# Loads cut into four pieces per partition row, and the tenth step's load and the constants issued earlier

## The chip, the core and the metric

The kernel runs on one core of one Trainium2 chip. The metric is the device time of one execution in microseconds (us), less is better. Its engines are named as in the profile: PE is TensorE's matmuls and PEld its weight loads, DVE is VectorE, ACT is ScalarE, POOL is GpSimd, SP is SyncE. Each engine works through its own instructions in order and waits on semaphores for the others. All loads and stores are issued by SP and carried by 16 DMA engines.

## What is computed

A retention layer (attention without softmax, with a decay of its own in each head) is followed by a feed-forward layer with softplus. Everything is float32:

```python
batch, n_heads, seq, head_dim = (8, 8, 576, 64)          # q, k, v
scores = q @ k.transpose(0, 1, 3, 2) / sqrt(64)
gamma = 1.0 - 2.0 ** (-5.0 - arange(8))
ret = scores * where(rel >= 0, gamma[:, None, None] ** rel, 0.0)   # rel = i - j
x = (ret @ v).transpose(0, 2, 1, 3).reshape(4608, 512)
h = x @ w_in                                             # w_in 512 x 2048
g = maximum(h, 0.0) + log1p(exp(-abs(h)))
return g @ w_out                                         # w_out 2048 x 512
```

## The kernel before

The 4608 tokens are cut into 36 chunks of 128. A **step** m is half of a chunk (four of the eight heads), so there are 72 steps, counted from 0. A step needs 576 KB of q, k and v in one tile, `raw0`, `raw1` and so on (`load_step`, line 118; step 0 comes as two `part` tiles together with constants). A step does `scores` and `sums` on PE (lines 156 and 169), the masked copy `a` and the running states on DVE (lines 178 to 210), then `values` on PE (lines 220 and 231), and `values_out`: x on DVE, its high part on ACT (line 246) and the rest on DVE or POOL (line 247). `scale_values` multiplies v by the decay, on ACT in the steps 0 to 8 (line 148) and on POOL from step 9 on (line 145).

The feed-forward layer goes over 9 units of 512 tokens (8 steps each) and in a unit over 16 slots of 128 hidden columns. A slot i is 12 matmuls `h` (`hidden_mm`, line 262), ACT's abs, exp and ln (lines 270 to 272), DVE's softplus (line 276) and the split of g into two parts (ACT line 280, DVE line 284), and 12 matmuls `y` (`output_mm`, line 296), which stand one slot later. Every product is made of three, from the high and the low parts of both sides.

The weights are 32 pieces of 512 KB (two for each p: w_in and w_out), loaded as float64 bits into `wst` (four buffers, `load_weight`) and turned into float32 high and low parts by `weight_p` (ACT, line 329), `weight_t` and `weight_b` (DVE, lines 336 and 342), `weight_c` (ACT, line 350) and `weight_d` (DVE, line 355). The load of piece n + 4 stands behind `weight_d(n)`.

The order is written by hand. **The opening** does the steps 0 to 8 (`AHEAD` is 9). All their loads and the weight pieces 0 to 3 are issued ahead of its loop; pieces 4 and 5, the loads of steps 9 and 10 and the full constants (`consts_sb`) are issued inside it. SP's loads share eight semaphores, `DMAHW0` to `DMAHW7`, so that each load waits until the one eight places ahead of it has landed. Behind the opening stands slot 0, whose `h` needs the x of steps 0 to 7. Slot 1 and every second slot after it begin with one more step on PE (step 9 in slot 1), ahead of the slot's `h`. The `h` of slot 1 needs weight piece 2, whose low part `weight_d(2)` makes on DVE during slot 0. DVE's order there is `weight_t(2)`, `weight_b(2)`, `weight_t(3)`, `weight_b(3)`, `weight_t(4)`, `weight_d(2)`, softplus.

Of the kernel before, what the change touches and what calls it, by code (L numbers as in the profile page):

```python
# [30 lines left out]
AHEAD = CPU * NPAIR // 2 + 1  # L31
# [8 lines left out]
OPENING = 3  # L40
NOPEN = AHEAD + 2
FIRST_HALF = NF // 2
WBUFS = 4
NPIECE = 2 * NF
HI, LO = 0, 1
# [15 lines left out]
def retention_softplus_ffn(ctx: ExitStack, tc, first, others, consts, w, out):  # L61
    nc = tc.nc
# [8 lines left out]
    openp = open_pools.enter_context(tc.tile_pool(name="openp", bufs=1))  # L71
    wst = weight_pools.enter_context(tc.tile_pool(name="wst", bufs=WBUFS, side="right"))
    later = {}
# [10 lines left out]
    consts_sb = const.tile([P, NCONST], F32, name="consts_sb")  # L84
# [11 lines left out]
    def place_weights(pool, upto):  # L96
        while len(ws) < upto:
            ws.append(pool.tile([P, 2, 2 * PIECE], F32R, name=f"w{len(ws)}"))

    place_weights(wpool, FIRST_HALF)  # L100

# [16 lines left out]
    def load_step(m):  # L118

        if m == 0:  # L120
            at = 0
            for x in parts:
                nc.sync.dma_start(x, first[:, at:at + x.shape[1]])
                at += x.shape[1]
            kq, kv = parts[0][:, 0:KQ], parts[1][:, 0:4 * C]
        else:
            if m < NOPEN:
                r = openp.tile([P, RAW], F32, name=f"raw{m}")
            else:
                r = rawp.tile([P, RAW], F32, tag="rawp", name="rawp")  # L130
            nc.sync.dma_start(r, others[m - 1])
            kq, kv = r[:, 0:KQ], r[:, KQ:]
        k = kq[:, 0:2 * C].rearrange("p (s c) -> p s c", s=2)
        q = kq[:, 2 * C:].rearrange("p (s c) -> p s c", s=2)
        kv = kv.rearrange("p (a s c) -> p a s c", a=2, s=2)
        live[m] = dict(k=k, q=q, kp=kv[:, 0], v=kv[:, 1])

    def scale_values(m):

        if m >= NSTEP:  # L140
            return
        v = live[m]["v"].rearrange("p s (h d) -> p (s h) d", h=2)
        f = constant[0][0][:, 4 * (m % 2):4 * (m % 2) + 4]
        if m >= AHEAD:
            nc.gpsimd.tensor_mul(v, v, f.unsqueeze(2).broadcast_to([P, 4, D]))  # L145
            return
        for n in range(4):
            nc.scalar.activation(v[:, n], v[:, n], AF.Copy, scale=f[:, n:n + 1])

    def scores(m, bank):  # L150
        if m >= NSTEP:
            return
        L = live[m]
        for s in range(2):
            for t, h in quads:
                nc.tensor.matmul(bank[rows[t], h, SCOLS][:, part[s]], L["k"][rows[h], s, part[t]],  # L156
                                 L["q"][rows[h], s, part[t]], start=True, stop=True, skip_group_check=True)
        L["bank"] = bank

    def sums(m):  # L160

        if m >= NSTEP:
            return
        L = live[m]
        start, follows = _chunk_kind(m // 2)
        for s in range(2):
            for t, h in quads:
                if follows if t else start != HC:
                    nc.tensor.matmul(L["bank"][rows[h], t, TCOLS][:, part[s]], L["kp"][rows[t], s, rows[h]],  # L169
                                     L["v"][rows[t], s, rows[h]], start=True, stop=True, skip_group_check=True)  # L170

    def scores_out(m):

        if m >= NSTEP:
            return
        L = live[m]
        a = moe.tile([P, 2, 2, HC], F32, tag="a", name="a")
        nc.vector.tensor_mul(a.rearrange("p h s c -> p (h s) c"),  # L178
                             L["bank"][:, :, SCOLS].rearrange("p h (s c) -> p h s c", s=2),
                             mask.unsqueeze(1).broadcast_to([P, 4, HC]))  # L180
        L["a"] = a
# [33 lines left out]
    def values(m, bank):  # L215

        L = live[m]
        for s in range(2):
            for t, h in quads:
                nc.tensor.matmul(bank[rows[h], t, VCOLS][:, part[s]], L["v"][rows[t], s, rows[h]],  # L220
                                 L["a"][rows[t], h, s], start=(s == 0), stop=L["states"][t] is None,
                                 skip_group_check=True)
        for s in range(2):
            for t, h in quads:
                if L["states"][t] is None:
                    continue
                if t == h:
                    lhs, rhs = L["states"][t], L["q"][rows[t], s, part[t]]
                else:
                    lhs, rhs = L["sx"], L["q"][rows[t], s, C:QC]  # L230
                nc.tensor.matmul(bank[rows[h], t, VCOLS][:, part[s]], lhs[rows[t], s], rhs, start=False, stop=True,  # L231
                                 skip_group_check=True)

    def values_out(m, bank, rest):

        live.pop(m)
        ch, pr = m // 2, 2 * (m % 2)
        cols = slice((ch % CPU) * C, (ch % CPU + 1) * C)
        hi, lo = (x_tile(ch // CPU)[:, n, pr:pr + 2, cols] for n in (HI, LO))
        x = att.tile([P, 2, C], F32, tag="x", name="x")  # L240
        nc.vector.tensor_mul(x.rearrange("p s (t c) -> p s t c", t=2),  # L241
                             bank[:, :, VCOLS].rearrange("p t (s c) -> p s t c", s=2),
                             constant[0][2][:, pr:pr + 2].rearrange("p s (t c) -> p s t c", t=2))

        def parts_out():
            nc.scalar.copy(hi, x)  # L246
            rest.tensor_sub(lo, x, hi.bitcast(F32))  # L247
        return parts_out
# [65 lines left out]
    wl = {}  # L314

    def load_weight(n):
        if n < NPIECE:
            wl[n] = wst.tile([P, PIECE, 2], I32, tag="wst", name="wst", bufs=WBUFS)
            nc.sync.dma_start(wl[n].rearrange("p c a -> p (c a)"), w[n // 2, n % 2])

    def weight_a(n):
        weight_p(n)
        weight_t(n)
# [14 lines left out]
    def weight_b(n):  # L338
        if n >= NPIECE:
            return  # L340
        hi, lo = wl[n][:, :, 1], wl[n][:, :, 0]
        nc.vector.scalar_tensor_tensor(hi, hi, 3, lo, op0=ALU.logical_shift_left, op1=ALU.bitwise_or)  # L342
# [5 lines left out]
    def weight_c(n):  # L348
        if n in wl:
            nc.scalar.copy(weight_dst(n)[0], wl[n][:, :, 1].bitcast(F32))  # L350

    def weight_d(n):
        if n in wl:
            head, rest = weight_dst(n)
            nc.vector.tensor_sub(rest, wl.pop(n)[:, :, 1].bitcast(F32), head.bitcast(F32))  # L355

    def weight_dl(n):
        if n in wl:
            weight_d(n)
            load_weight(n + WBUFS)  # L360

# [4 lines left out]
    for m in range(AHEAD):  # L366
        load_step(m)
        for n in first_weights.get(m, ()):
            load_weight(n)
    nc.gpsimd.memset(mask, 1.0)  # L370
    for n in range(2):
        nc.gpsimd.affine_select(out=mask[rows[n]], in_=mask[rows[n]], pattern=[[1, HC]], compare_op=ALU.is_ge,
# [7 lines left out]
    for m in range(AHEAD):  # L380
        pair = ps_open.tile([P, 2, T], F32, tag="pair", name="pair")
        bank = (ps_val if m % 2 else ps_att).tile([P, 2, T], F32, tag="val" if m % 2 else "bank", name="bank")
        if m < AHEAD - 1:
            scores(m, pair)
            sums(m)
        if m > 0:
            values(m - 1, bank)
        if m == AHEAD - 1:
            scores(m, pair)
            sums(m)  # L390
            values_out(m - 1, bank, nc.vector)()
        if m < AHEAD - 1:
            scale_values(m + 1)
        scores_out(m)
        states_out(m)
        if 0 < m < AHEAD - 1:
            values_out(m - 1, bank, nc.gpsimd)()
        if m in (3, 6):
            weight_b((m - 3) // 3)
            weight_c((m - 3) // 3)  # L400
        if m in (4, 7):
            weight_d((m - 4) // 3)
            load_weight((m - 4) // 3 + WBUFS)
        if m in (2, 5, 8):
            weight_a((m - 2) // 3)
        if m == AHEAD - 2:
            load_step(AHEAD)
            nc.sync.dma_start(consts_sb, consts)
            load_step(AHEAD + 1)
    weight_b(2)  # L410
    scale_values(AHEAD)
# [6 lines left out]
    for i in range(NSLOT):  # L418
        n = START_WEIGHTS + 2 * i
        m = AHEAD + (i - 1) // 2  # L420
# [115 lines left out]
```

## Time and profile before

| | us |
|---|---|
| median of three runs | 905.57 (904.87 to 907.06) |
| the profiled execution | 907.14 |
| its span, first to last instruction | 905.4 |
| PE busy in the span | 889.3 (98%) |
| PE idle in the first 40 us | 11.0 |

The profiled execution took 907.14 us, of which the span is 905.4 us. The page lists each engine's busy time, the slices of the span, the DMA queues, and a chain of work that ended last. In the chain PE holds 92%, DVE 4%, DMA 2% and ACT 1%. A table by stretch tells where PE does not work, a timeline of an engine tells what each wait ended with ("<-"), and the DMA view tells what the queues carried in a stretch: queue q1 carries the kernel's loads and stores, q8 and q14 carry instructions. In these profiles a matmul of float32 operands stands as two rows of work, and "issue" is time in which the engine waited for nothing that the profile shows.

### The profile page before, as it was taken

The page shows a single profiled execution, that of the slowest core. Times are in us where ns is not written, and L with a number is a line of the kernel's source. Part 1 is how long each engine was busy: PE and PEld are TensorE (multiplying, and loading weights), DVE is VectorE, ACT ScalarE, POOL GpSimd, SP SyncE. Part 2 cuts the span into 40 slices and gives each one's busy share as a digit, 9 for nine tenths or more (in the row PEclk, how much of TensorE's full clock was granted, in tenths as well). Part 3 has the DMA queues.
Part 4 walks back from the last instruction along what each step waited for, and adds up shares of the span by engine and source line. Part 5 has one row for each costly group of instructions (what it writes and reads, how often), then busy time and mean ns, then how long its engine had stood idle before and what let it go on. Part 6 is the DMA issues. An engine that isn't in the chain of part 4 may idle for free.

```text
span 905.4 us, 18152 instructions
## 1 busy us (share of the span) xinstructions
PE 889.3 (98%) x7826; PEld 724.9 (80%) x7826; DVE 366.4 (40%) x742; ACT 443.3 (49%) x771; POOL 144.9 (16%) x269
## 2 busy tenths in 40 slices
PE   6899999999999999999999999999999999999998
PEld 5677778888888888888888888888888888888886
DVE  5788963333332343333333333323332432332222
ACT  5687764344444444444444444444444444445444
POOL 3312211111111111111111111111111111100000
PEclk9899999999999999999999999999999999999999
DMA  9565623111211131111211131113111121101001
GB/s 362 185 206 199 211 81 100 53 54 54 98 33 49 54 100 54 54 52 38 90 54 53 54 100 53 30 51 101 53 54 54 64 67 50 54 1 47 1 1 46
DMA packets 20527, 70.37 MB, mean 78 GB/s; under 512 B 2272, under 2 KB 2272, under 8 KB 20448
## 3 DMA queue, kind: packets, MB, share of 16 engines
q1 hardware_dynamic: 20448, 69.23, 22.9%
q8 instruction: 61, 1.00, 0.5%
q14 instruction: 18, 0.15, 0.0%
HBM read 59.78 MB, written 9.44 MB: 76 GB/s over the span
## 4 chain that ended last, share of the span: by engine, by line
PE 92%; DVE 4%; DMA 2%; ACT 1%; issue 1%; SPq 0%; DVEq 0%
PE h L262 43%; PE y L296 41%; PE bank L156 3%; PE bank L220 2%; PE bank L231 2%; PE bank L169 2%; DMA raw<-others 1%; DVE w L355 1%; DVE g L284 1%; DMA wst<-w 0%; DVE x L241 0%; DVE a L178 0%; ACT ab L272 0%; ACT ab L271 0%; ACT ab L270 0%
## 5 line engine op out<-in xcount | busy, mean ns | idle before, releaser
L262 PE MATMUL h<-xt,w 128*128 128x512 f32 (+1 forms) x1740 | 426.7, 395 | 0.0
L296 PE MATMUL y<-w,g 128*128 128x512 f32 x1728 | 415.8, 390 | 1.3 <-DVE g L284 1.3
L296 PEld LDWEIGHTS y<-w,g 128*128 128x128 f32 x1728 | 324.0, 188 | 70.7 <-DVE g L284 3.8
L262 PEld LDWEIGHTS h<-xt,w 128*128 128x128 f32 x1740 | 321.8, 189 | 69.1 <-ACT xt L246 0.6
L276 DVE SCALAR_TENSOR_TENSOR ab<-h,ab 128x512 f32<-128x512 f32 (+1 forms) x145 | 99.8, 688 | 427.2 <-ACT ab L272 427.2
L270 ACT ACTIVATE ab<-h 128x512 f32<-128x512 f32 (+1 forms) x145 | 86.3, 595 | 257.6 <-PE h L262 257.6
L280 ACT CAST g<-ab 128x512 fp32r<-128x512 f32 (+1 forms) x145 | 89.5, 617 | 102.5 <-DVE ab L276 101.3
L284 DVE TENSOR_TENSOR g<-ab,g 128x512 fp32r<-128x512 f32 (+1 forms) x145 | 101.3, 699 | 90.6 <-ACT g L280 89.2
L247 POOL TENSOR_TENSOR xt<-x,xt 128x256 fp32r<-128x256 f32 x71 | 54.6, 769 | 470.8 <-ACT xt L246 470.5
L271 ACT ACTIVATE ab<-ab 128x512 f32<-128x512 f32 (+1 forms) x145 | 91.2, 629 | 4.6
L272 ACT ACTIVATE ab<-ab 128x512 f32<-128x512 f32 (+1 forms) x145 | 91.2, 629 | 4.6
L246 ACT CAST xt<-x 128x256 fp32r<-128x256 f32 x72 | 29.2, 406 | 68.3 <-DVE x L241 68.3
L145 POOL TENSOR_TENSOR rawp<-rawp,consts_sb 128x256 f32<-128x256 f32 x61 | 39.9, 655 | 110.2 <-DMA rawp<-others 110.2
L156 PEld LDWEIGHTS bank<-rawp 64*64 64x64 f32 x976 | 19.8, 133 | 21.5 <-issue 21.5
L212 POOL TENSOR_TENSOR s<-s,consts_sb 128x128 f32<-128x128 f32 x55 | 23.9, 435 | 60.5 <-DVE s L210 49.3
L156 PE MATMUL bank<-rawp 64*64 64x64 f32 x976 | 28.2, 231 | 0.0
L350 ACT CAST w<-wst 128x512 fp32r<-128x512 f32 x32 | 21.2, 663 | 13.5 <-DVE wst L342 13.3
L220 PE MATMUL bank<-a,rawp 64*64 64x64 f32 x976 | 27.3, 220 | 0.0
L241 DVE TENSOR_TENSOR x<-bank,consts_sb 128x256 f32<-128x256 f32 x64 | 26.7, 418 | 0.0
L178 DVE TENSOR_TENSOR a<-bank,mask 128x256 f32<-128x256 f32 x63 | 26.2, 416 | 0.0
L231 PE MATMUL bank<-rawp,sx 64*64 64x64 f32 x440 | 25.2, 218 | 0.0
L169 PE MATMUL bank<-rawp 64*64 64x64 f32 x864 | 25.2, 218 | 0.0
(70 smaller groups left out, 411.2 us busy)
## 6 DMA issues: line engine op xcount, KB each, us to landing
rawp<-others SPq DMA_DIRECT2D x61, 576.0 KB, 4.0
wst<-w SPq DMA_DIRECT2D x32, 512.0 KB, 4.1
out<-osb SPq DMA_DIRECT2D x36, 256.0 KB, 2.4
raw<-others SPq DMA_DIRECT2D x10, 576.0 KB, 8.8
part<-first SPq DMA_DIRECT2D x1, 512.0 KB, 3.7
part<-first SPq DMA_DIRECT2D x1, 326.0 KB, 2.9
consts_sb<-consts SPq DMA_DIRECT2D x1, 262.0 KB, 5.8
```

The lines of the kernel that those rows point to most:

```text
L156: nc.tensor.matmul(bank[rows[t], h, SCOLS][:, part[s]], L["k"][rows[h], s, part[t]], L["q"][rows[h], s, part[t]], start=True, stop=True, s ...
L169: nc.tensor.matmul(L["bank"][rows[h], t, TCOLS][:, part[s]], L["kp"][rows[t], s, rows[h]], L["v"][rows[t], s, rows[h]], start=True, stop=T ...
L220: nc.tensor.matmul(bank[rows[h], t, VCOLS][:, part[s]], L["v"][rows[t], s, rows[h]], L["a"][rows[t], h, s], start=(s == 0), stop=L["states ...
L247: rest.tensor_sub(lo, x, hi.bitcast(F32))
L262: nc.tensor.matmul(h, ws[p][:, a, kt * P:(kt + 1) * P], xt[:, b, kt, cols], start=(n == 0), stop=(n == 3 * NKT - 1))
L270: nc.scalar.activation(ab, h, AF.Abs)
L271: nc.scalar.activation(ab, ab, AF.Exp, scale=-1.0)
L272: nc.scalar.activation(ab, ab, AF.Ln, bias=1.0)
L276: nc.vector.scalar_tensor_tensor(ab, h, 0.0, ab, op0=ALU.max, op1=ALU.add)
L280: nc.scalar.copy(g[:, HI], ab)
L284: nc.vector.tensor_sub(g[:, LO], ab, g[:, HI].bitcast(F32))
L296: nc.tensor.matmul(y, g[:, a, at:at + P], ws[p][:, b, PIECE:], start=(p == 0 and n == 0), stop=(p == NF - 1 and n == 2))
```

## The change

Two things are changed.

Each step's load from `others` and each weight piece from `w` is laid out in DRAM as four pieces, each of which holds a quarter of every partition's row. A load still is one DMA instruction into the same tile, but a partition's 4608 bytes (4096 for weights) come as four runs of 1152 (1024) bytes.

The load of step 9 (`AHEAD`) and that of `consts_sb` move from the loop of the opening to a place ahead of it, behind the opening's loads. The load of step 10 stays where it was.

```diff
+ROWS = 4
...
-            nc.sync.dma_start(r, others[m - 1])
+            nc.sync.dma_start(r.rearrange("p (a c) -> p a c", a=ROWS), others[m - 1].rearrange("a p c -> p a c"))
...
-            nc.sync.dma_start(wl[n].rearrange("p c a -> p (c a)"), w[n // 2, n % 2])
+            nc.sync.dma_start(wl[n].rearrange("p (r c) a -> p r (c a)", r=ROWS),
+                              w[n // 2, n % 2].rearrange("r p c -> p r c"))
...
         load_step(m)
         for n in first_weights.get(m, ()):
             load_weight(n)
+    load_step(AHEAD)
+    nc.sync.dma_start(consts_sb, consts)
     nc.gpsimd.memset(mask, 1.0)
...
         if m == AHEAD - 2:
-            load_step(AHEAD)
-            nc.sync.dma_start(consts_sb, consts)
             load_step(AHEAD + 1)
...
+    def in_rows(a):
+        return np.moveaxis(a.reshape(a.shape[:-1] + (ROWS, -1)), -2, -3)
...
-        "others": np.concatenate([kq[1:], kv[1:]], axis=2),
+        "others": in_rows(np.concatenate([kq[1:], kv[1:]], axis=2)),
...
-        "w": np.stack([w_in, w_out], axis=1),
+        "w": in_rows(np.stack([w_in, w_out], axis=1)),
```

SP's instructions before, from the load of step 8 on, at the end of the opening's loads; `raw9` is the tenth step, the `wst` rows are the weight pieces 3, 4, 5 and (last) 6, and DVE_49 is the wait for `weight_d`:

```order
L131 DMA raw8_127<-others 128x1152 [waits DMAHW4_49]
L319 DMA wst_129<-w 128x1024 [waits DMAHW5_49]
L319 DMA wst_378<-w 128x1024 [waits DMAHW6_49,DVE_49]
L319 DMA wst_541<-w 128x1024 [waits DMAHW7_49,DMAHW0_49,DVE_49]
L131 DMA raw9_543<-others 128x1152
L408 DMA consts_sb_93<-consts 128x524 [waits DMAHW1_49]
L131 DMA raw10_546<-others 128x1152 [waits DMAHW2_49]
L319 DMA wst_624<-w 128x1024 [waits DMAHW3_49,DVE_49]
```

Before, `raw9` stands behind pieces 4 and 5 and so behind two waits for DVE. The same place of SP after the change:

```order
L132 DMA raw8_127<-others 128x4x288 [waits DMAHW4_49]
L320 DMA wst_129<-w 128x4x256 [waits DMAHW5_49]
L132 DMA raw9_131<-others 128x4x288 [waits DMAHW6_49]
L373 DMA consts_sb_93<-consts 128x524 [waits DMAHW7_49]
L320 DMA wst_381<-w 128x4x256 [waits DMAHW0_49,DVE_49]
L320 DMA wst_544<-w 128x4x256 [waits DMAHW1_49,DVE_49]
L132 DMA raw10_546<-others 128x4x288 [waits DMAHW2_49]
L320 DMA wst_624<-w 128x4x256 [waits DMAHW3_49,DVE_49]
```

`raw9` and the constants now wait for earlier loads alone, and pieces 4 and 5 stand behind them. PE, DVE, ACT and POOL have the same instructions in the same order as before.

## Rows read from the trace of the kernel before

**Rows 1.** The page: busy us (share) xinstructions; queue: packets, MB, share of 16 engines.

```profile
PE 889.3 (98%) x7826; PEld 724.9 (80%) x7826; DVE 366.4 (40%) x742; ACT 443.3 (49%) x771; POOL 144.9 (16%) x269
...
q8 instruction: 61, 1.00, 0.5%
```

**Rows 2.** Busy time by stretch: us, busy (x instructions) per engine, PEclk, DMA share, GB/s.

```profile
10.00:20.00 10.00, 6.16 (x237) 5.40 (x232) 8.88 (x26) 7.20 (x24) 6.39 (x13) 0.89 1.02 416
...
200.00:300.00 100.00, 100.00 (x877) 81.66 (x876) 34.34 (x71) 45.77 (x77) 17.29 (x33) 1.00 0.18 59
```

**Rows 3.** The same view, from the start up to PE's two gaps.

```profile
0.00:14.90 14.90, 10.46 (x221) 8.45 (x222) 6.95 (x22) 8.10 (x25) 4.58 (x15) 0.89 0.89 341
0.00:20.80 20.80, 13.37 (x348) 10.94 (x349) 11.59 (x34) 12.47 (x39) 8.34 (x22) 0.92 0.93 362
```

**Rows 4.** PE's timeline: start us, us, line, tile, count [idle before <- what ended it].

```profile
15.00 0.35 PE L156 MATMUL pair<-raw 64*64 64x64 f32 x9 [1.52 <-issue]
...
20.90 0.39 PE L156 MATMUL pair<-raw 64*64 64x64 f32 x10 [2.95 <-issue]
...
25.93 4.70 PE L262 MATMUL h<-xt,w 128*128 128x512 f32 x12
32.66 0.69 PE L156 MATMUL bank<-raw 64*64 64x64 f32 x16 [2.04 <-DMA raw<-others]
...
34.38 3.83 PE L262 MATMUL h<-xt,w 128*128 128x512 f32 x12
...
43.49 2.88 PE L296 MATMUL y<-w,g 128*128 128x512 f32 x12
```

**Rows 5.** DMA queues in 12.57 to 12.59, 18.56 to 18.58 and 22.52 to 22.54 us.

```profile
q8 instruction: 1, 0.02, 292.5%
...
q8 instruction: 1, 0.02, 301.2%
...
q8 instruction: 1, 0.02, 287.5%
```

**Rows 6.** DMA queues, packets of one size: 12.11:12.41 (4608 B), 30.71:30.86 (2096), 901.2:901.7 (2048).

```profile
q1 hardware_dynamic: 30, 0.14, 111.2%
...
q1 hardware_dynamic: 26, 0.05, 93.5%
...
q1 hardware_dynamic: 85, 0.17, 94.9%
```

**Rows 7.** SP's timeline: start and length of the issues of step 8, pieces 4 and 5, step 9.

```profile
10.08 0.33 SPq L131 DMA_DIRECT2D raw<-others  x1
...
18.03 8.50 SPq L319 DMA_DIRECT2D wst<-w  x2
26.58 0.72 SPq L131 DMA_DIRECT2D raw<-others  x1
```

**Rows 8.** DMA issues at 10.08 and at 18.03 us: KB each, us from issue to landing.

```profile
raw<-others SPq DMA_DIRECT2D x1, 576.0 KB, 11.4
...
wst<-w SPq DMA_DIRECT2D x1, 512.0 KB, 6.0
```

**Rows 9.** DVE's timeline around slots 0 and 1 (columns as in PE's).

```profile
26.98 0.43 DVE L247 TENSOR_TENSOR xt<-x,xt 128x256 fp32r<-128x256 f32 x1 [0.47 <-ACT xt L246]
...
30.13 0.42 DVE L336 TENSOR_SCALAR wst<-wst 128x512 int32<-128x512 uint32 x1
30.47 0.69 DVE L355 TENSOR_TENSOR w<-wst,w 128x512 fp32r<-128x512 f32 x1
32.61 0.69 DVE L276 SCALAR_TENSOR_TENSOR ab<-h,ab 128x512 f32<-128x512 f32 x1 [1.46 <-ACT ab L272]
```

**Rows 10.** ACT's timeline in the same stretch.

```profile
24.52 1.07 ACT L148 ACTIVATE raw<-raw,part 128x64 f32<-128x64 f32 x4
...
35.33 0.68 ACT L350 CAST w<-wst 128x512 fp32r<-128x512 f32 x1 [0.20 <-DVE wst L342]
38.25 0.60 ACT L270 ACTIVATE ab<-h 128x512 f32<-128x512 f32 x1 [2.25 <-PE h L262]
```

## The prediction
> **What bounds the kernel now.** I read the busy times first: PE is at work for 889.3 of 905.4 us [rows 1], and in the steady stage for all of it, 100.00 of 100 us [rows 2]. The transfers there take 0.18 of the DMA engines' time, so dearer ones do not hold PE up. What the change can move is the head, where PE is idle for 11 of the first 40 us. From about 2 to 22 us the DMA engines are full (share 1.02, 416 GB/s) [rows 2], so there a transfer lands when the ones ahead of it have been carried.
>
> PE's timeline shows three gaps that matter [rows 4]. At 15.00 and 20.90 it resumes after 1.52 and 2.95 us in which it waited for nothing that the profile shows, in the middle of the scores of steps 4 and 6. At 32.66 it resumes after 2.04 us of waiting for the load of step 9.
>
> The first two have a cause in the DMA view, I think. Queue q8 carried 61 packets of together 1.00 MB [rows 1], 16.4 KB each; PE and PEld have 15,652 instructions, 257 for each packet. Up to the two gaps they had done 221 + 222 = 443 and 348 + 349 = 697 [rows 3], 254 apart. So PE stops at the ends of blocks of instructions, and q8 carries the next block. The next packet of q8 starts at 12.57 and the one after at 18.56 [rows 5]; by its share (292.5% of 16 engines for 0.02 us) it takes 0.94 us, and PE resumes 1.4 to 1.5 us behind its end. If a block is asked for when PE enters the one before it, the second was asked for at 15.00 and its packet began 3.57 us later. The third, asked for at 20.90, began 1.63 us later (22.53), when the data queues were running empty. The difference, 1.9 us, is a wait behind data, about eleven packets of 178 ns.
>
> **Part 1, the moved load.** SP issues pieces 4 and 5 at 18.03 and later; the second waits for `weight_d(1)`, and step 9 is issued behind it at 26.58 [rows 7]. PE ends the first `h` at 25.93 + 4.70 = 30.63 and stands until 32.66; the `h` of slot 1 starts at 34.38 [rows 4]. After the change step 9 needs only `raw4` landed and lands long before 30 us (below), and so do the constants. That takes away 2.04 us directly. POOL's scaling of the step's v, which followed the landing too, then lies under the first `h`, and the step's block on PE (34.38 - 32.66 = 1.72 us) becomes no longer. What is late next is `weight_d(2)`, at 30.47 to 31.16 [rows 9].
>
> The two moved transfers cost something too: on the DMA engines they stand ahead of piece 4, whose `weight_t(4)` DVE does at 30.13, just ahead of `weight_d(2)`.
>
> **Part 2, the price of a packet.** A 4608-byte packet takes 178 ns (16 engines x 0.3 us x 1.112 / 30), a 2096-byte one 86.3, a 2048-byte one of a store 89.3 [rows 6]. A line through the two loads has 9.8 ns for each packet and 36.5 ns for a KB of 1000 bytes: 1152 bytes take 51.9 ns, 1024 bytes 47.2. On one engine a step's load is 8 x 178 = 1.42 us before and 32 x 51.9 = 1.66 after, a weight piece 1.27 and 1.51: 0.24 us more each. A line through the load of 4608 and the store gives 18.3 ns a packet, 58.3 and 53.8 ns, and 0.45 us more each. I take the lower price, since both its rows are loads, and keep the other for the range. In this stretch no row shows that cut packets could be cheaper than whole ones: both lines have a price per packet.
>
> The load of step 8 landed at 10.08 + 11.4 = 21.5 and piece 4 at 18.03 + 6.0 = 24.0 [rows 7, 8]. Ahead of step 8's landing stand 11 cut transfers (steps 1 to 8, pieces 0 to 2): 21.5 + 11 x 0.24 = 24.1 (26.4 at the dear price). Piece 4 has 13 of them with its own, and now step 9 (1.66) and the constants (8 x 0.086 = 0.69) ahead of it: 24.0 + 3.1 + 1.66 + 0.69 = 29.5 (32.4). Step 9 itself lands 2.2 us ahead of that, at 27.3 (29.8), in time for PE at 30.
>
> The Trainium skill ("DMA: Bandwidth & Descriptors", "Why small descriptors are slow (HBM only)") gives some 3 cycles for a packet beside one per 32 bytes; by it the cut costs a step's load 6%, 0.09 us. The rows of this trace show about three times that. With the page's price piece 4 would land at 27.4 and the time would be near 901.6, inside the range below.
>
> **Part 3, the block of instructions.** The 1.9 us of waiting is eleven packets. Packets of 52 ns would make it 0.6, and a block comes 1.3 us sooner. Counted back from step 8's landing by what one engine carries, step 6 landed at 21.5 - 1.42 - 1.27 - 1.42 = 17.4 and step 4 at 13.3; with eight and five cut transfers that is 19.3 and 14.5 now. The first block arrives at 15.00 - 1.3 = 13.7, ahead of step 4's data; the second is asked for at 14.5 and arrives 5.9 - 1.3 = 4.6 later, at 19.1, ahead of step 6's. Both gaps go, and the loads take their place: PE does step 6 at 19.3 instead of 20.90, but step 8 at 24.1. What the gaps gave in this head is paid back in part by part 2.
>
> **The sum.** From step 8's landing at 24.1: ACT scales its v (1.07 us) [rows 10], then makes two high parts of x (0.4 us each, half overlapped), so DVE's last rest of x, which the first `h` needs and which began at 26.98 [rows 9], begins at about 26.0, 1.0 us sooner. The first `h` ends at 29.6 instead of 30.63, the block of step 9 at 29.6 + 1.7 = 31.3 or, at a lower cost, 30.7. DVE reaches `weight_t(4)` at 29.1 and waits for piece 4 until 29.5; `weight_d(2)` ends at 30.5 instead of 31.16. So the second `h` starts at 30.7 to 31.3 instead of 34.38: 3.1 to 3.7 us sooner. Behind it ACT must follow: its cast of line 350 (35.33) follows softplus of slot 0 (32.61) by 2.7 us; with softplus at 31.6 that cast ends at 35.0, and abs of slot 1, at 38.25 before [rows 10], starts at 35.0 to 35.2. So ACT is 3.1 us sooner. Of PE's `y` of slot 1, at 43.49 before, I then expect 3.1 to 3.7 us less, and say 3.5. Later each weight load is 0.24 us longer; I take 0.3 us off for a DVE that waits for one of the last pieces. **3.2 us** is left. At the dear price piece 4 lands at 32.4, the second `h` starts at 33.3, slot 1's ACT gains 1.3, and 1.1 is left. At the good end, with the page's cheap packet or a full clock in the second `h` (3.83 us in the trace, 2.88 for a `y` later [rows 4]), it is 4.2.
>
> Against the profiled execution that is 907.14 - 3.2 = 903.9 (span 902.2). The median of the runs is 1.57 lower, 905.57, and the same difference gives 902.4 (901.4 to 904.5).
>
> **Rival: the block waits for transfers, not for packets.** For it: 1.9 us is also 1.3 whole transfers; a queue that is left only at a transfer's end, or a lookahead counted in bytes, gives the same gaps. Against it: the third wait, 1.63 us, fell short where packets were few. The blocks then come 1.9 x 0.24 / 1.42 = 0.3 us later each, and later requests add up: PE resumes step 6 at 22.1 instead of 20.90, the first `h` ends at 31.9, step 9's block at 33.2 to 33.6 (gain 0.8 to 1.2 at the second `h`), and softplus of slot 0 moves out by as much as PE. About 1.3 is left, 1.0 with the later weights: **904.6**. The Trainium skill ("DMA: Bandwidth & Descriptors", "Queues, rings and completion order") says that a DMA engine changes queues only between packets of typically 9 to 17 descriptors, which would be a whole transfer's share of an engine here; by that rule this rival is the case. The trace cannot tell, since its packets are counted one by one.
>
> **Rival: SP's issue grows with the pieces, and the time ends above before.** Place: SP's queue ahead of 25 us. All issues of the trace have 128 runs and took 0.33 to 0.72 us [rows 7]; with 512 runs the price lies between 0.33 (nothing) and 4 x 0.72 = 2.88. It decides from where a load's issue is slower than its carrying, 1.66 us; the gain is gone when piece 4 comes 4 us later than in my sum, over 14 transfers 0.29 each, so at 1.95 us an issue. At 2.88 piece 4 lands 17 us late, 13 us are lost behind the gain's end: **918.6**. For it: only that no row shows such an issue. Against it: both ends of the issue times shown are those of the same kind of load, so what stretches an issue there is not its size.
>
> **How the numbers follow.** Forecast 0.60: the rows of three fetches speak for packets. Block waits for transfers 0.28. Slow issue, or a packet above 61 ns (which has the same point of decision), 0.12. A measurement of this kernel tells about 0.3%, 2.7 us, from no change, so the line lies at 902.9. Of the forecast 0.7 lies below it (its own range is 901.4 to 904.5), of the second case almost nothing, 0.01: faster 0.43. Slower 0.14: the third case and a little of the second. The same 0.43. The range reaches from 901.2 to 905.6; it leaves out the third case and the ends of the others, under 0.2.
>
> **What would show it.** In the profile after, the DMA lines should have 4 x as many data packets for loads and about 52 ns for one; step 8 should land near 24 and piece 4 near 29.5. PE should have no "issue" gap above 0.5 us ahead of 25 us, and a gap that ends with DMA in its place; with gaps that stay at 1.5 to 3 us the second case holds. No PE wait should end with `raw9`; DVE's `weight_t(4)` should wait shortly for piece 4. The second `h` should start at 30.7 to 31.3, and the `y` of slot 1 near 40. I am wrong if SP's issues are above 1.5 us, if the loads land later than at the dear price, or if what is won by 43 us is given back in the weights' stage up to 130 us.

## The result and the profile after

The changed kernel takes 909.67 us (median of 6 runs, 907.95 to 910.41) against 905.96 (904.87 to 907.06) for the kernel before in the same six rounds: 3.7 us more, a ratio of 1.0037 [1.0022, 1.0051]. The forecast was 902.4 us, 3.2 us faster, with a range up to 905.6. It had the wrong sign, and the time lies outside the range.

The profiled execution took 909.83 us, 2.69 more than that of before (907.14). All of it is lost in the head. From the `h` of slot 16 on, the two executions run in step: that `h` starts at 131.99 instead of 129.30 us, and 776.13 us are left behind it in both. So everything below is about the first 40 us.

PE's timeline after (start us, us, line, tile, count, idle before and what ended it), which answers to [rows 4]:

```profile
15.48 0.35 PE L157 MATMUL pair<-raw 64*64 64x64 f32 x9 [1.27 <-issue]
...
21.96 0.58 PE L157 MATMUL pair<-raw 64*64 64x64 f32 x10 [2.63 <-issue]
...
28.43 0.58 PE L221 MATMUL bank<-a,raw 64*64 64x64 f32 x9 [2.18 <-issue]
...
30.32 5.00 PE L263 MATMUL h<-xt,w 128*128 128x512 f32 x12
35.25 0.46 PE L157 MATMUL bank<-raw 64*64 64x64 f32 x16
36.17 3.01 PE L263 MATMUL h<-xt,w 128*128 128x512 f32 x12
...
45.55 3.02 PE L297 MATMUL y<-w,g 128*128 128x512 f32 x12 [0.33 <-DVE g L285]
...
131.99 2.88 PE L263 MATMUL h<-xt,w 128*128 128x512 f32 x12
```

The last wait of [rows 4], 2.04 us for the load of step 9, is gone: at 35.25 PE goes on without a pause. But the two "issue" gaps are still there, and behind them there is a third, 2.18 us before 28.43, in the values of step 7 (line 221). The waits of PE by releaser between 28 and 62 us have it as their only entry of this kind:

```profile
PE bank L221 <- issue: 2.2, 1, 2.2
```

The first `h` starts at 30.32 instead of 25.93, 4.39 us late, and takes 5.00 us instead of 4.70.

Busy time by stretch (columns as in [rows 2, 3]), from the start up to each of the three gaps:

```profile
0.00:15.30 15.30, 10.39 (x221) 8.63 (x222) 6.62 (x22) 7.78 (x24) 4.44 (x15) 1.00 0.93 325
0.00:21.80 21.80, 13.94 (x348) 11.75 (x349) 11.60 (x34) 13.08 (x41) 8.72 (x23) 0.90 0.98 340
0.00:28.30 28.30, 17.99 (x476) 15.43 (x476) 16.09 (x46) 15.55 (x48) 11.49 (x29) 0.81 0.93 322
```

PE and PEld had done 443 and 697 instructions at the first two gaps, as before [rows 3], and 952 at the third, 255 on. The rate up to the second gap is 340 GB/s; it was 362.

The DMA queues at the start of the instruction packets behind the three gaps (windows of 0.02 us from 12.99, 19.39 and 25.84 us):

```profile
q8 instruction: 1, 0.02, 329.1%
...
q8 instruction: 1, 0.02, 350.3%
...
q8 instruction: 1, 0.02, 376.2%
```

Read as in [rows 5], the packets took 1.05, 1.12 and 1.20 us. The second block, asked for at 15.48, has its packet begin at 19.40, 3.92 us later (before 3.57); the third, asked for at 21.96, begins at 25.85, 3.89 us later (before 1.63). That third packet is what the change made late.

The loads and the price of their packets: the queue in two stretches with packets of one size (10.81 to 11.31 us: 1152 B; 44.4 to 44.9: 1024 B), then the loads issued at 13.96 (step 8) and 20.15 us (piece 4) with the time from issue to landing.

```profile
q1 hardware_dynamic: 173, 0.20, 110.3%
...
q1 hardware_dynamic: 192, 0.20, 110.4%
```

```profile
raw<-others SPq DMA_DIRECT2D x1, 576.0 KB, 9.2
...
wst<-w SPq DMA_DIRECT2D x1, 512.0 KB, 8.2
```

A packet takes 16 x 0.5 x 1.103 / 173 = 51.0 ns and 46.0 ns. Step 8 landed at 13.96 + 9.2 = 23.2 us, piece 4 at 20.15 + 8.2 = 28.3. The full engines carried 380 GB/s from 10 to 20 us, where before it was 416 [rows 2]:

```profile
10.00:20.00 10.00, 6.82 (x254) 6.03 (x248) 8.75 (x27) 7.11 (x24) 6.26 (x13) 0.88 1.09 380
```

DVE's and ACT's timelines after, which answer to [rows 9, 10]:

```profile
34.45 0.68 DVE L357 TENSOR_TENSOR w<-wst,w 128x512 fp32r<-128x512 f32 x1
37.31 0.69 DVE L277 SCALAR_TENSOR_TENSOR ab<-h,ab 128x512 f32<-128x512 f32 x1 [2.18 <-ACT ab L273]
...
40.58 0.60 ACT L271 ACTIVATE ab<-h 128x512 f32<-128x512 f32 x1
```

Softplus of slot 0 comes at 37.31 instead of 32.61, 4.70 us late. From it to the `h` of slot 16 the kernel before needed 129.30 - 32.61 = 96.69 us and the changed one 131.99 - 37.31 = 94.68. So the change does give 2.01 us behind softplus, and loses 4.70 ahead of it.

### The profile page after: what moved, and what is told of

Its sections match the earlier page's. It is cut to its first block, busy times and chain, and to the rows that moved or that the text cites. A ratio compares the mean times of both kernels' runs of the same rounds, so it can differ in the third digit from the quotient of the medians.

```text
span 908.1 us, 18152 instructions
## 1 busy us (share of the span) xinstructions
PE 891.6 (98%) x7826; PEld 726.8 (80%) x7826; DVE 366.2 (40%) x742; ACT 443.2 (49%) x771; POOL 143.7 (16%) x269
## 4 chain that ended last, share of the span: by engine, by line
PE 91%; DVE 4%; ACT 2%; issue 1%; DMA 1%; POOL 0%; SPq 0%; POOLq 0%; DVEq 0%
PE h L263 42%; PE y L297 41%; PE bank L157 3%; PE bank L221 2%; PE bank L232 2%; PE bank L170 2%; DMA raw<-others 1%; DVE g L285 1%; DMA wst<-w 1%; DVE w L357 1%; ACT ab L273 0%; ACT ab L272 0%; PE pair L170 0%; ACT ab L271 0%; DVE a L179 0%
## 5 line engine op out<-in xcount | busy, mean ns | idle before, releaser
L179 DVE TENSOR_TENSOR a<-bank,mask 128x256 f32<-128x256 f32 x63 | 26.2, 415 | 0.0
```

## Experiments

The theory formed on these rows: the third block of PE's instructions is asked for at about 21 us. Before, the data queue ran dry soon after that, at about 22.5 us. Both edits make it run dry later, and the block waits until it does. The rivals are the size of a packet (a block waits for a number of packets), the slow issues of SP, the half clock of the first `h`, and the chance that a block's end falls at a bad place. Ratios are against the kernel before, with 95% intervals. "Third packet" is the start of the instruction packet for the third block.

**The move alone, in whole rows.**

```
     for n in first_weights.get(m, ()): load_weight(n)
+load_step(AHEAD)
+nc.sync.dma_start(consts_sb, consts)
...
     if m == AHEAD - 2:
-        load_step(AHEAD)
-        nc.sync.dma_start(consts_sb, consts)
```

> Whole rows as before; the load of step 9 and the constants stand behind the opening's loads, as in the change. Theory A (the moved loads fill the DMA queue when PE asks for its third block of instructions): the block that comes at 24.8 us before now comes 1.5 to 2.5 us later, with an issue gap of about 2 us behind step 7, the first h starts near 28 and the second near 34; the time is within 1 us of before. Theory B (the cut packets alone cost the time, the move gains): no third gap above 0.5 us, the second h starts near 31.7, the time is 2 to 3 us lower.

Measured: 907.16 us, 1.0006 [0.9995, 1.0016]. PE's timeline:

```profile
26.95 0.38 PE L220 MATMUL bank<-a,raw 64*64 64x64 f32 x9 [1.78 <-issue]
...
28.57 4.00 PE L262 MATMUL h<-xt,w 128*128 128x512 f32 x12
33.44 2.79 PE L262 MATMUL h<-xt,w 128*128 128x512 f32 x11
```

The third gap is there without any cut row. The third packet starts at 24.54 us instead of 22.53, and the first `h` at 28.57 instead of 25.93. The wait for step 9 is gone; softplus of slot 0 is 1.95 us late (34.56), and from it to the `h` of slot 16 it is 94.39 us instead of 96.69. The move gains 2.30 us and loses 1.95; no change of the time is shown.

**The cut alone, loads at their old places.**

```
-            nc.sync.dma_start(r, others[m - 1])
+            nc.sync.dma_start(r.rearrange("p (a c) -> p a c", a=ROWS),
+                              others[m - 1].rearrange("a p c -> p a c"))
```

(and the weights' load likewise)

> Four pieces per row, the load of step 9 and the constants where they were. Theory A: the first two gaps end 0.5 and 1.1 us later than before, the third block comes about as long after the second as before (3.9 us), the wait for step 9 stays; the time is 1 to 1.6 us above before. Theory B: all of the change's loss and the gain of the move on top, 4 us or more above before.

Measured: 908.04 us, 1.0025 [1.0011, 1.0040]. PE's timeline:

```profile
21.80 0.59 PE L157 MATMUL pair<-raw 64*64 64x64 f32 x10 [2.58 <-issue]
...
26.34 0.58 PE L221 MATMUL bank<-a,raw 64*64 64x64 f32 x9 [0.26 <-issue]
...
28.24 4.33 PE L263 MATMUL h<-xt,w 128*128 128x512 f32 x12
32.97 0.46 PE L157 MATMUL bank<-raw 64*64 64x64 f32 x16 [0.41 <-DMA raw<-others]
34.24 2.11 PE L263 MATMUL h<-xt,w 128*128 128x512 f32 x8
```

The cut by itself makes the kernel slower. The second block waited 3.80 us, not less; the third packet starts at 23.80, and PE stands only 0.26 us for it: at a granted clock of 0.50 (1.2 GHz) from 21 us on it came to the end of the second block late itself (before, the clock was 1.00 up to 25 us). The first `h` is 2.31 us late, but of the second nothing is left (34.24 against 34.38 [rows 4]), since the wait for step 9 shrinks from 2.04 to 0.41 us: that wait had hidden the lateness. This profiled execution is only 0.8 us longer in its span than that of before (906.2 against 905.4), less than the ratio says (2.3 us). It loses all of this behind the head: at the `h` of slot 3 it is 0.53 us ahead (46.85 against 47.38), but from there to the `h` of slot 16 it takes 83.25 us, before 81.92, and PE has a wait there for a step's load (window 46 to 130 us) that the kernel before does not have:

```profile
PE bank L157 <- DMA rawp<-others: 0.5, 1, 0.5
```

What the other runs lost beyond that, no trace shows.

The two ratios add to 1.0031, the whole change has 1.0037 [1.0022, 1.0051]: no sign that the edits need each other.

**The moved loads behind piece 4.** Whole rows; step 9 and the constants are issued in the loop at m = 7, ahead of piece 5 instead of behind it.

```
+            if m == 7:
+                load_step(AHEAD)
+                nc.sync.dma_start(consts_sb, consts)
```

> Whole rows; the load of step 9 and the constants stand behind weight piece 4 and ahead of piece 5, with no wait of their own. They are issued at about 18.5 us, so they are queued when the third block is asked for (20.9). Theory A: the third block is late by 1.5 to 2.5 us as in the run with the move alone, time within 1 us of before. Theory B: no third gap, 2 to 3 us below before.

Measured: 907.22 us, 1.0009 [0.9998, 1.0020]. Nothing holds SP there: step 9 goes out at 18.46 us all the same, so it is in the queue when the third block is asked for (21.18), as in the move alone. SP's timeline:

```profile
18.46 0.43 SPq L131 DMA_DIRECT2D raw<-others  x1
18.94 1.28 SPq L405 DMA_DIRECT2D consts_sb<-consts  x1
```

The third packet starts at 24.50 and PE resumes at 26.81. So it is not piece 4's place in the queue that makes the third block late. No change of the time is shown here either.

**The same place, held back by a buffer.** Step 9 takes step 6's tile, so its issue waits for the last reader of that step and the queue runs dry first.

```
-                r = openp.tile([P, RAW], F32, name=f"raw{m}")
+                n = 6 if m == AHEAD else m
+                r = openp.tile([P, RAW], F32, tag=f"raw{n}", name=f"raw{n}")
```

> Whole rows; the same place on SP, but step 9 is loaded into the buffer of step 6, so that it is issued only when PE has done that step's values, at about 22.8 us, behind the request for the third block and ahead of the wait for DVE. Theory A: no third gap above 0.5 us, step 9 is there at about 27, PE does not wait for it, the second h starts near 31.8: 2 to 3 us below before and as much below the run with the same place and no wait. Theory B: the same time as that run.

Measured: 904.29 us, **0.9972 [0.9959, 0.9984]**, faster than both kernels. SP's and PE's timelines:

```profile
25.28 0.33 SPq L132 DMA_DIRECT2D raw<-others  x1
```

```profile
21.63 0.58 PE L157 MATMUL pair<-raw 64*64 64x64 f32 x10 [2.98 <-issue]
...
27.44 3.24 PE L263 MATMUL h<-xt,w 128*128 128x512 f32 x12
30.61 0.46 PE L157 MATMUL bank<-raw 64*64 64x64 f32 x16
32.75 3.04 PE L263 MATMUL h<-xt,w 128*128 128x512 f32 x12 [1.14 <-DVE w L356]
...
126.98 2.88 PE L263 MATMUL h<-xt,w 128*128 128x512 f32 x12
```

Step 9 goes out at 25.28 us (22.8 was expected), 1.30 ahead of [rows 7], lands at 29.85, and PE does not wait for it. The third gap is gone: the third packet starts at 22.74, 1.1 us after it was asked for. Between this kernel and the one before it lies only the time at which step 9, and behind it on SP the constants and piece 5, are issued; the ratios are 0.9972 and 1.0009. The clock has a part in this one trace: the granted clock was back at 1.00 (2.4 GHz) from 28 us on, the first `h` took 3.24 us instead of 4.70, and it ended where it did before (30.68 against 30.63) although it began 1.51 later. What this is worth over all runs stands below.

**The same with cut rows.**

> Four pieces per row with the load of step 9 in the buffer of step 6 (issued when PE is done with that step). It is the price of the cut where no wait for step 9 hides it. Theory A: the first h 1.5 to 2.3 us later than with whole rows at this place, and about 1 us more lost in the stage of the weights: 2.5 to 3.5 us above that run, so about 0.5 us above before. Rival: the cut costs 1 to 2 us as it does with the load at its old place; 1 us below before.

Measured: 906.37 us, 1.0002 [0.9986, 1.0017]. By the two ratios (1.0002 and 0.9972) the cut costs about 0.30% here, 2.7 us; alone it costs 0.25%. The first `h` is 0.89 us later than with whole rows, less than expected, and nothing more is lost behind the head. PE's timeline has the third gap again, smaller:

```profile
26.44 0.58 PE L222 MATMUL bank<-a,raw 64*64 64x64 f32 x9 [1.09 <-issue]
...
28.33 3.83 PE L264 MATMUL h<-xt,w 128*128 128x512 f32 x12
```

The reason stands in busy time by stretch (last columns: granted clock, DMA share, GB/s). First the held-back load in whole rows, from 22 to 24 us, then the same with cut rows, from 22 to 25:

```profile
22.00:23.00 1.00, 1.00 (x50) 1.00 (x48) 0.32 (x1) 0.00 (x0) 0.00 (x0) 0.50 0.60 234
23.00:24.00 1.00, 1.00 (x48) 1.00 (x44) 0.94 (x5) 0.00 (x0) 0.00 (x0) 0.50 0.13 53
```

```profile
22.00:23.00 1.00, 1.00 (x48) 1.00 (x48) 0.84 (x3) 0.00 (x0) 0.00 (x0) 0.50 1.09 354
23.00:24.00 1.00, 1.00 (x48) 1.00 (x44) 0.97 (x4) 0.25 (x1) 0.40 (x1) 0.50 1.06 332
24.00:25.00 1.00, 0.79 (x28) 0.60 (x23) 1.00 (x3) 0.65 (x2) 0.77 (x1) 0.50 0.21 65
```

With whole rows the engines run dry at about 22.6 us, with cut rows at about 24: they carry the same bytes at a lower rate (332 to 354 GB/s here; from 10 to 20 us 380, where whole rows had 416 [rows 2]). The third packet starts at 22.74 and at 23.73. The clock is 0.50 (1.2 GHz) in all these rows, so it does not tell the two apart.

**Cut rows behind the opening only.** Steps 1 to 10 and pieces 0 to 5 in whole rows, the rest cut.

> Whole rows for the steps 1 to 10 and the weight pieces 0 to 5, four pieces per row for all later ones; the order of before. If the cut loses time in the stage of the weights (the loads there are 0.15 to 0.24 us longer each), the starts of h are as before up to slot 2 and 0.8 to 1.3 us later at slot 16; the time 0.8 to 1.3 us above before. If the loss is the opening's alone, no slot is later and the time is the same.

Measured: 907.40 us, 1.0008 [0.9992, 1.0024]. Inconclusive: a cost of 0.1% in the weights' stage can neither be shown nor ruled out. In its trace the `h` of slot 16 is not later (129.22 us against 129.30). The head's blocks were as before (second wait 3.68 us).

**Two pieces instead of four, loads at their old places.**

> The kernel before with two pieces per row (runs of 2304 and 2048 bytes), one transfer per load as before. It has the packets of the run with halves, but half as many transfers, in flight up to eight of twice the size. The second block's packet began 3.6 us after the end of the gap ahead of it with whole rows, 3.8 to 3.9 with four pieces, 2.9 with halves. If it is the length of the transfers (or the bytes that SP has in flight) that the block waits for, 3.6 to 3.8 us here; if it is the packet's size, 2.9. The time 0.5 to 1.5 us above before.

Measured: 906.51 us, 0.9995 [0.9980, 1.0011], no change. The second block waited 3.68 us behind packets of 2304 B. Behind 4608 B it waited 3.57 in the kernel before [rows 4, 5] and 3.62 to 3.83 in the five other kernels with whole rows in the opening, and behind 1152 B 3.80 to 3.92 in the three kernels with four pieces. The wait is not a number of packets, and these ranges are too close to say that it grows with cut rows.

**Each load as two transfers of half the columns** (kernel before otherwise; then with the held-back step 9; then that with halves for the opening's loads alone).

```
+            for c in (slice(0, RAW // 2), slice(RAW // 2, RAW)):
+                nc.sync.dma_start(r[:, c], others[m - 1][:, c])
```

(and the weights' pieces likewise)

> The kernel before with every step's load and weight piece issued as two transfers of half the columns (rows of 2304 and 2048 bytes). Asks what PE's wait for its block of instructions is counted in. Second block, from the end of the gap ahead of it to the start of its packet: 3.57 us before. If the wait is counted in packets (11 of them), about 2.4 us; if in transfers, about 2.4 us too; if in bytes on the engine, 3.5 to 3.8 us, and both gaps stay. The time: 1.5 us below before if it is short, 0 to 2 us above if it is not.

> All loads issued as two transfers of half the columns, and the load of step 9 in the buffer of step 6. Theory: the blocks come 0.6 us sooner each and PE does not wait for step 9, so the second h starts at 30.5 to 32 (32.75 with whole transfers): 3 to 4.5 us below before. Rival: twice the transfers through eight places delay the weights' stage by as much, 2 to 3 us below before, as with whole transfers.

> As the run with halves and the late load of step 9, but only the loads of the opening (steps 1 to 8, pieces 0 to 3) are halves; all later ones are whole. Theory: the same early start of the second h (30.5 to 32), and the weights' stage as in the kernel before: 3 to 4.5 us below before. Rival: the halves give nothing by themselves, 2 to 3 us below.

Measured: 907.48 us, 1.0013 [0.9997, 1.0029]; 906.87 us, 1.0002 [0.9988, 1.0015]; 906.33 us, 0.9995 [0.9983, 1.0008]. The second block waited 2.86, 3.81 and 3.26 us. If the wait were a number of transfers, half transfers would halve it in all three. They do not; nor is it fixed. None of the gains that were expected came (1.5 us for short waits; 3 to 4.5 us, or 2 to 3 by the rivals, with the held-back load), and none of the three beats the held-back load in whole rows. A third gap is in each, 1.68, 0.73 and 1.68 us, also with the load held back: PE asked for the third block at 20.01 to 20.64 us, and its packet started at 23.00 to 23.60, when the queue ran dry.

**The blocks shifted.** Eight unused matmuls of 64x64x64 at the start of PE's program.

```
+    for n in range(8):
+        nc.tensor.matmul(idle[0:D, 0, 0:D], fill[0:D, 0:D], fill[0:D, 0:D], start=True, stop=True)
```

> The kernel before with 8 small matmuls (64x64x64, 32 rows of PE work) added behind the three of the start, where PE waits for the first load; their results are not used. If the gaps are ends of blocks of instructions, PE stops again at the same count of its instructions (443 and 697 counted so far), so 32 earlier in the steps: in step 3's values instead of step 4's scores, and in step 5's values instead of step 6's scores. If the gaps belong to those steps' loads, they stay in the scores of steps 4 and 6 and the counts rise by 32. Time within 1.5 us of before.

Measured: 905.49 us, 0.9991 [0.9976, 1.0007]. PE's timeline, and busy time up to the gaps:

```profile
15.89 0.27 PE L231 MATMUL bank<-raw,s 64*64 64x64 f32 x1 [1.89 <-issue]
...
21.89 0.27 PE L231 MATMUL bank<-raw,u 64*64 64x64 f32 x1 [1.81 <-issue]
```

```profile
0.00:15.50 15.50, 12.07 (x222) 10.49 (x222) 6.27 (x20) 7.82 (x24) 4.62 (x15) 1.00 0.88 337
0.00:21.50 21.50, 16.08 (x349) 14.17 (x349) 10.70 (x32) 11.14 (x35) 7.51 (x21) 0.92 0.91 357
```

The gaps stay at 444 and 698 instructions and move to other lines of the program (L231, the values, instead of the scores). They belong to the count, not to an operation: they are ends of blocks of instructions. That it matters to the time where in a step they fall is not shown.

## Why the prediction was wrong

The main kernels side by side (us from the start; "stands" is PE's issue gap ahead of the third block, "rest" the time from softplus of slot 0 to the `h` of slot 16):

| kernel | step 9 issued | third packet | stands | first `h` | rest | ratio |
|---|---|---|---|---|---|---|
| before | 26.58 | 22.53 | - | 25.93 | 96.69 | 1 |
| move alone | 13.26 | 24.54 | 1.78 | 28.57 | 94.39 | 1.0006 |
| moved, behind piece 4 | 18.46 | 24.50 | 1.55 | 27.88 | 94.48 | 1.0009 |
| moved, held back | 25.28 | 22.74 | - | 27.44 | 94.23 | 0.9972 |
| cut alone | 27.92 | 23.80 | 0.26 | 28.24 | 95.54 | 1.0025 |
| the change, held back | 24.73 | 23.73 | 1.09 | 28.33 | 94.20 | 1.0002 |
| the change | 17.18 | 25.85 | 2.18 | 30.32 | 94.68 | 1.0037 |

**What the third block waits for.** Its packet starts when the data queue runs dry. With whole rows and step 9 at its old place it starts at 22.53 us, with the move alone at 24.54 (2.01 later), with the cut alone at 23.80 (1.27 later). The sum of both puts it at 22.53 + 2.01 + 1.27 = 25.81; the changed kernel has 25.85 (each from one execution). The engines' load in the changed kernel, microsecond by microsecond:

```profile
24.00:25.00 1.00, 1.00 (x48) 1.00 (x44) 1.00 (x3) 0.36 (x1) 0.40 (x1) 0.50 1.07 386
25.00:26.00 1.00, 0.78 (x26) 0.59 (x19) 0.97 (x4) 0.64 (x3) 0.84 (x1) 0.50 1.10 353
26.00:27.00 1.00, 0.24 (x6) 0.06 (x3) 0.97 (x4) 1.00 (x6) 0.60 (x2) 0.50 0.27 93
```

The share falls from 1.10 to 0.27 around 26 us, where the packet starts. The block needs that packet's 1.20 us and about 1.4 more, and PE goes on at 28.43. Before, it went on with this block at 24.79, about 1.3 us behind the end of its packet:

```profile
24.79 0.33 PE L220 MATMUL bank<-a,raw 64*64 64x64 f32 x5
```

So the block is 3.64 us late. That is most of the 4.39 us by which the first `h` is late and of the 4.70 us at softplus of slot 0. That this is the cause, and not only beside it, is shown by the held-back load: step 9 is still there when PE needs it, but it is not in the queue at 21 us, and the ratio falls from 1.0009 to 0.9972 with whole rows and from 1.0037 (the change) to 1.0002 with cut ones. One thing stays open: the wait of 3.89 us is as long as that of the second block (3.92), which ended with the queue full, so no run shows whether a queue that is full for longer would hold the third block for longer.

**Part 3, the block of instructions: the step that failed.** I took the wait as eleven packets, so that packets of 52 ns would make it 0.6 us instead of 1.9. It did not shrink: in all it was 3.57 us before and 3.92 after, and three sizes of packets give 3.57 to 3.83, 3.68 and 3.80 to 3.92. "Both gaps go" was wrong: both stayed (1.27 and 2.63 us). The evidence that I leaned on, the short third wait of 1.63 us "where packets were few", meant that the queue was running empty; it said nothing about the size of a packet.

**Parts 1 and 2, what was left out.** I charged the two moved transfers to piece 4 and to nobody else. But my own sum kept the DMA engines busy up to the landing of piece 4 at 29.5 us, and the third block was asked for at about 21. [Rows 5] show three instruction packets; I worked out the new wait of two of them and not of the third, which the two extra transfers hit: its wait went from 1.63 to 3.89 us, and its packet from 22.53 to 25.85.

**Part 1, the gain: right.** PE no longer waits for `raw9`, and the part behind softplus of slot 0 is shorter by 2.01 us (2.30 with the move alone), against 2.04 us of removed wait [rows 4]. In every kernel with step 9 issued ahead of piece 5 it is 94.2 to 94.7 us to the `h` of slot 16, whatever came before; with the load at its old place 95.2 to 98.3. So the gain behind softplus did not depend on how late softplus was.

**Part 2, the price: right in kind, and smaller than summed.** 51.9 and 47.2 ns were worked out, 51.0 and 46.0 measured. Step 8 landed at 23.2 (24.1 by the sum), piece 4 at 28.3 (29.5), step 9 at 26.2 (27.3). By the packets' times a step's load takes an engine 32 x 51.0 - 8 x 178 = 0.21 us longer, 8.7 ns a packet beside the bytes. But those times overlap more with cut rows (share 1.09 against 1.02), and by the rate, 380 against 416 GB/s, the load costs 9%, about 0.13 us (an estimate); step 8 was 1.7 us late behind 11 cut transfers, 0.15 each. The Trainium skill ("DMA: Bandwidth & Descriptors", "Why small descriptors are slow (HBM only)") has some 3 cycles for a packet, 6% of a step's load by the prediction. The 9% of this trace is more than that, but nearer to it than the 17% of my sum (0.24 of 1.42 us).

But I made nothing of the price beyond the loads themselves. The cut costs 0.25% alone and about 0.30% beside the held-back load. In the head the third packet starts 1.0 to 1.3 us later with it, and PE stood 0.26 and 1.09 us for that block; what the rest of the cost is made of is not shown.

**The second `h`** was to start at 30.7 to 31.3 and started at 36.17. The first `h` took 5.00 us; PE's granted clock was 0.50 (1.2 GHz) in the rows above up to 27 us (before, it was 1.00 from 20 to 25 us), and with the held-back load the same twelve matmuls took 3.24. So a lower clock lengthened the head of this execution too. It does not carry the result: over the 35 runs of the kernel before beside the first experiments, the time is 0.35 us lower for each 0.001 more of mean granted clock. Their mean is 0.9943, that of the changed kernel's six runs 0.9928, that of the held-back load's twelve 0.9954. By this estimate the clock is about 0.5 us of the 3.7 lost, and 0.4 us of the 2.7 won.

**The rival "the block waits for transfers"** was right that the gaps stay; its check ("gaps that stay at 1.5 to 3 us") came nearly true (1.27 and 2.63 us). It had the wrong sign as well: its 904.6 us was too low by 5 us, and it too had no third block. Whether transfers, bytes or something else are counted is open: halves gave 2.86, 3.81 and 3.26 us. The Trainium skill ("DMA: Bandwidth & Descriptors", "Queues, rings and completion order") has a DMA engine change queues between packets of 9 to 17 descriptors. One engine carries 8 descriptors of a whole load and 32 of a cut one, so by that rule a cut load could be left half way; the waits with cut rows, 3.80 to 3.92 us against 3.57 to 3.83 with whole ones, do not bear that out.

**The rival "SP's issue grows with the pieces"** was half right. Issues by tile (least, median and longest ns, first and last us), and the issue of step 8 on SP's timeline, which took 0.33 us before [rows 7]:

```profile
L132 SPq DMA_DIRECT2D raw<-others x10: 427/1416/2460, 1.7 to 28.1; - x10
```

```profile
13.96 1.70 SPq L132 DMA_DIRECT2D raw<-others  x1
```

The median was 433 ns before. In the full queue, from 4 to 19 us, the issues of cut loads took 1.31 to 2.46 us, some of them above the 1.5 us that I had named as a sign of being wrong; whole ones took 0.33 us in the same stretch of the kernel before from 7 us on. With room in the queue a cut load took 0.50 (28.08 us). The median stays under the 1.66 us at which I let it decide, the engines stayed full (share 1.09), and the loads landed earlier than my sum, not later. So it did not decide.

**What stays open:** what the second block's wait counts, why halves give three values for it, and how much the cut costs in the weights' stage. From the `h` of slot 3 to that of slot 16 the cut alone took 1.33 us more than before and the changed kernel 0.48 more, but the cut with the held-back load took as long as before.

## What to carry to other kernels

When the DMA engines are full, ask what else needs them: the instructions of a busy PE come over the same engines, a block of some 255 matmuls and weight loads at a time, and a load issued early can hold back the very engine that it is to serve. Find those packets in the trace, write down when each block is asked for, and keep the queue empty at that point; a buffer that delays an issue by some us (step 9 in step 6's tile) can be worth more than an earlier issue (0.9972 here, where the earlier issue alone gave 1.0006). A removed wait is worth its length only if what comes ahead of it is not made later: here 2 us were won behind softplus and 4.7 lost ahead of it.

## What the runs showed of the hardware that was not expected

- The wait of an instruction packet behind a full queue hardly depends on the size of the data packets: 3.57 to 3.83 us at 4608 B, 3.68 at 2304 B, 3.80 to 3.92 at 1152 B. It is cut short when the queue runs dry: 1.1 and 1.63 us.
- The second instruction packet, carried while the engines are full, took 0.95 to 0.99 us in the six kernels with whole rows in the opening and 1.08 to 1.14 in the three with four pieces.
- Cut rows lower the rate of full engines: 380 GB/s from 10 to 20 us, 416 before [rows 2].
- With the queue full, one issue of a cut load on SP took 1.31 to 2.46 us, one of a whole load 0.33 (from 7 us on); with room in the queue a cut one took 0.37 to 0.50 (changed kernel).
